# Linear attention and a two-layer product: q of the late batches transposed by DMA instead of TensorE

## The chip, the cores and the metric

The kernel runs on one core of one Trainium2 chip. The metric is the time of one execution on the device in microseconds; the kernel before takes 289.67 us (median of 3 runs, 289.25 to 289.86). The profiled execution has a span of 288.3 us, and TensorE's granted clock is 1.0 throughout.

A core has five engines that run their own instruction streams in order and meet at semaphores: TensorE (PE, matrix products into PSUM), VectorE (DVE), ScalarE (ACT), GpSimd (POOL) and SyncE (SP). Transfers between memory and the on-chip SBUF are issued from POOL, SP or ACT and carried out by 16 DMA engines that all three share. POOL's transfers can change the type on the way; here they read fp32 and write fp16.

## The reference

Eight batches of 576 tokens, 8 heads of 64. Attention without softmax, a normalisation per head, then a two-layer product with a leaky activation over all 4,608 tokens:

```python
kv = np.einsum('bhsd,bhse->bhde', k, v)
out = np.einsum('bhsd,bhde->bhse', q, kv)
rms = np.sqrt(np.mean(out * out, axis=-1, keepdims=True) + 1e-06)
attn = out / rms * g_norm                  # then (B, S, H*D) -> x: 4608 x 512
h = x @ w_in                               # 512 x 2048
g = np.maximum(h, 0.0) + alpha * np.minimum(h, 0.0)
y = g @ w_out                              # 2048 x 512
```

## The kernel before

**Windows, blocks, units.** The 4,608 tokens are cut into nine windows of 512. The loop `for w in range(1, NW)` (L731) has one block for each window from 1 to 8; window 0 is done in the start-up. A block has 16 units. In each unit TensorE computes one group of 128 hidden columns of the first layer for window w (`m1_group`, L368: four products of 512 columns), seven products of 256 columns of the second layer for window w-1 (`prod_mm`, L478; the second layer is done by a scheme with seven half-size products in place of eight), and now and then a step of the attention for window w+1 (`attention`, L713). All orders are written by hand: the schedule is manual, so each engine runs its instructions in the order in which the Python code makes them.

**Attention.** A batch has 576 tokens, a window 512, so a window touches one or two batches. Heads go in four pairs (j = 0 to 3). `step_t` (L263) transposes q of a pair: five TensorE transposes of 128x128 into a PSUM bank, then an ACT copy to SBUF (L282). `step_kv` (L284) adds up k times v over the batch's tokens into the bank "s" and DVE writes the masked result. `step_ot` (L301) multiplies k-v with the transposed q for the window's tokens; ACT squares it. `step_ssq` (L319) sums the squares and scales, giving the input `xt` of the first layer. In block w, the t step of batch w+1 stands at units 0, 3, 6 and 9, kv one unit later, ot at 3, 6, 9 and 12 and ssq two units after ot (`ATT_AT`, L701).

**Evacuation.** A first-layer group goes from PSUM through ACT (`m_sb`, L359) and DVE (`gt`, L363). From block 2 on there are two PSUM banks for the groups, so TensorE's group u+2 needs DVE to have finished group u.

**Loads.** `load_batch(w + 2)` (L731 and following) issues on POOL, for k, v and q of batch w+2: the last 64 tokens of each head (`load_rem`, L148) straight to their place in one of three sets of buffers, and the first 512 (`load_main`, L140) to a staging tile with two buffers. In the staging tile partition p holds tokens 4p to 4p+3, so each packet carries four tokens of a head: 1 KB read, 512 B written. POOL runs ahead of the loop and stops only at a load whose buffer is not free; everything behind such a load waits too.

**Regroup.** k and q are copied from the staging tile to an order in which a pair of heads is contiguous, on ACT, one pair at a time in units 8 to 15 of block w for batch w+2 (`regroup_pair`, L174; `REG_AT`, L723: q of pair j at unit 8+2j, k at 9+2j).

**Stores.** Because q holds tokens in the order 4p+t, a run of 128 result rows is spread over the output with a step of four rows, and `store_rows` (L385) cuts it where t changes or the remainder begins. Results are read from PSUM in quarters of a window (`y_read`, L509: c11 after unit 7, c22 after 11, c21 after 14, c12 in the next block's unit 0) into `y_sb`, four buffers, and stored from SP.

Of the kernel before, what the change touches and what calls it, by code (L numbers as in the profile page):

```python
# [10 lines left out]
FP16 = mybir.dt.float16  # L11
# [6 lines left out]
def kernel(  # L18
# [11 lines left out]
    nc = tc.nc  # L30

    B, H, S, D = q.shape
# [3 lines left out]
    P = 128  # L36
    NPAIR = H // 2
    W = 512
    NW = N_TOK // W
    TPW = W // P  # L40
    TPP = S // P
    MAIN = TPP * P
    REM = S - MAIN
    NT = TPP + 1
# [2 lines left out]
    NF = D_FF // P  # L47
    NC = D_MODEL // P
    assert NC == NPAIR and 0 < REM < P and P0 <= P and H % 4 == 0
    inv_d = 1.0 / D  # L50

    const_p = ctx.enter_context(tc.tile_pool(name="constp", bufs=1))
# [3 lines left out]
    stage_p = ctx.enter_context(tc.tile_pool(name="stage", bufs=2))  # L56
    attn_p = ctx.enter_context(tc.tile_pool(name="attn", bufs=2))
# [14 lines left out]
    srcs = {"q": q, "k": k, "v": v}  # L72
    st32 = {}

    def early_pair(eng, nm, tag):
# [14 lines left out]
            name=nc.get_next_instruction_name(),  # L90
# [20 lines left out]
    for r in range(P // D):  # L111
        nc.sync.dma_start(
            out=alpha_row[NF : NF + 1, r * D : (r + 1) * D], in_=g_norm[:].unsqueeze(0)
# [4 lines left out]
    NBUF = 3  # L118
    HH = H // 2
    bufs = []  # L120
    for i in range(NBUF):
        t = {}
# [6 lines left out]
    stages = {}  # L129
# [10 lines left out]
    def load_main(b, nm):  # L140
        st = stage_p.tile([P, H, TPP, D], FP16, name=f"{nm}st", tag=f"{nm}st")
        stages[b, nm] = st
        nc.gpsimd.dma_start(  # L143
            out=st[:].rearrange("p h t d -> p h (t d)"),
            in_=srcs[nm][b, :, 0:MAIN, :].rearrange("h (p t) d -> p h (t d)", t=TPP),
        )

    def load_rem(b, nm):  # L148
        nc.gpsimd.dma_start(
            out=bufs[b % NBUF][nm][0:REM, 0 if nm == "v" else TPP, :, :],  # L150
            in_=srcs[nm][b, :, MAIN:S, :].rearrange("h s d -> s h d"),
        )

    def regroup(b, nm, h0, h1, eng=None):
        dst = bufs[b % NBUF][nm][:, 0:TPP, h0:h1, :].rearrange("p t h d -> p h t d")
        src = stages[b, nm][:, h0:h1, :, :]
        if eng is nc.scalar:
            nc.scalar.copy(out=dst, in_=src)
        else:
            (eng or nc.vector).tensor_copy(out=dst, in_=src)  # L160

    def load_batch(b, names=("k", "v", "q")):
        for nm in names:
            load_rem(b, nm)
            load_main(b, nm)

    def regroup0(nm, j, n=1):
        i, h = divmod(2 * j, HH)
# [5 lines left out]
    def regroup_pair(b, nm, j):  # L174
        regroup(b, nm, 2 * j, 2 * j + 2, nc.scalar)
# [66 lines left out]
    qts, kvs, xts = {}, {}, {}  # L242

    def rows(b):
        return P0 if b == 0 else P

    def n_runs(b):
        return T0 if b == 0 else NT

    def pair_cols(b, nm, j):  # L250
        def f(t):
            n = rows(b)
            if nm == "v" and b == 0:
                h = 2 * j % HH
                return stages[b, nm, 2 * j // HH][0:n, h : h + 2, t, :]
            if nm == "v" and t < TPP:
                return stages[b, nm][:, 2 * j : 2 * j + 2, t, :]
            if nm == "v":
                return bufs[b % NBUF][nm][0:n, 0, 2 * j : 2 * j + 2, :]
            return bufs[b % NBUF][nm][0:n, t, 2 * j : 2 * j + 2, :]  # L260
        return f

    def step_t(b, j, pool=(ps_s, "s")):  # L263
        qs = pair_cols(b, "q", j)
        qt_ps = pool[0].tile([P, n_runs(b) * rows(b)], FP16, name="qt_ps", tag=pool[1])
        c = 0
        for t in range(n_runs(b)):
            n = rows(b)
            nc.tensor.matmul(  # L269
                out=qt_ps[:, c : c + n],  # L270
                lhsT=qs(t),
                rhs=ident16[0:n, 0:n],
                is_transpose=True,
                start=(t == 0),
                stop=(t == n_runs(b) - 1),
            )
            c += n
        qts[b, j] = attn_p.tile([P, S], FP16, name="qt_sb", tag=f"qt{j}")
        if b == 0 and j < 2:
            nc.vector.tensor_copy(out=qts[b, j][:], in_=qt_ps[:, 0:S])  # L280
        else:
            nc.scalar.copy(out=qts[b, j][:], in_=qt_ps[:, 0:S])  # L282

    def step_kv(b, j, pool=(ps_s, "s")):  # L284
        ks, vs = pair_cols(b, "k", j), pair_cols(b, "v", j)
# [82 lines left out]
    def m1_group(w, g, pool=None):  # L368
        h_ps = pool[0].tile([P, W], FP32, name="h_ps", tag=pool[1]) if pool else h_bank()
        m1_mm(h_ps, w, g, range(NC))  # L370
        m1_evac(h_ps, w, g)
# [4 lines left out]
    def y_mm(y, w, a, g):  # L376
        nc.tensor.matmul(  # L377
            out=y[:], lhsT=gt_cols(w, g, a * P, (a + 1) * P), rhs=w_out_blk(g),
            start=(g == 0), stop=(g == NF - 1),
        )  # L380

    store_engines = [(nc.gpsimd,)]
    store_turn = [0]

    def store_rows(n0, src, c0, c1):  # L385
        i = 0
        while i < P:
            b, r = divmod(n0 + i, S)
            np_, nt = (P0, T0) if b == 0 else (P, TPP)
            if r < np_ * nt:  # L390
                t, p = divmod(r, np_)
                cnt = min(P - i, np_ - p)
                grid = out[b * S : b * S + np_ * nt, :].rearrange("(p t) m -> t p m", t=nt)
                dst = grid[t, p : p + cnt, c0:c1]
            else:
                cnt = min(P - i, S - r)
                dst = out[b * S + r : b * S + r + cnt, c0:c1]
            engs = store_engines[0]
            store_turn[0] += 1
            engs[store_turn[0] % len(engs)].dma_start(out=dst, in_=src[i : i + cnt])  # L400
            i += cnt

    def y_out(y, w, a):
        y_sb = ysb_p.tile([P, D_MODEL], FP32, name="y_sb")
        nc.scalar.copy(out=y_sb[:], in_=y[:])
        store_rows(w * W + a * P, y_sb[:], 0, D_MODEL)


    HC = D_MODEL // 2
# [32 lines left out]
    HW = W // 2  # L442
# [60 lines left out]
        )  # L503

    def quad_out(w, r, h, src, subs=(0, 1)):
        for a in subs:
            store_rows(w * W + r * HW + a * P, src[:, a, :], h * HC, (h + 1) * HC)

    def y_read(w, what, subs=(0, 1)):  # L509
        if what == "p1":  # L510
# [47 lines left out]
    def h_at(i):  # L558
# [7 lines left out]
        out=alpha_ps[:], lhsT=alpha_row[0 : NF + 1, 0:P], rhs=ident[0 : NF + 1, 0 : NF + 1],  # L566
# [6 lines left out]
        out=beta_sb[:], in0=alpha_ps[:, 0:NF], scalar1=-1.0, scalar2=1.0, op0=ALU.mult, op1=ALU.add,  # L573
# [5 lines left out]
    regroup0("q", 1)  # L579
    keep_warm(1)  # L580
    step_t(0, 1, h_at(1))
    regroup0("k", 1)
    ssq_mm(0, 0)
# [112 lines left out]
    def unit_sums(w, u):  # L696
        for back, n, k in S_AT.get(u, ()):
            if 1 <= w + back < NW:
                s_sum(w + back, n, k)
# [13 lines left out]
    def attention(w, u):  # L713
        if w < NW:
            for what, j in (ATT_1 if w == 2 else ATT_AT).get(u, ()):
                if w < B or what in ("ot", "ssq"):
                    if w == 2 and what in ("kv", "ssq"):
                        pool = Q_POOL if j % 2 == 0 else S_POOL
                        (step_kv if what == "kv" else step_ssq)(w, j, pool)
                    else:  # L720
                        ATT[what](w, j)

    REG_AT = {8 + 2 * j + i: ((nm, j),) for j in range(NPAIR) for i, nm in ((0, "q"), (1, "k"))}  # L723

    Y3_AT = [(8, 8), (8, 8), (8, 8), (8, 9), (9, 9), (9, 10), (10, 10), (10, 10), (10, 11), (11, 11), (11, 12), (12, 12), (12, 13), (13, 14), (14, 15), (15, 16)]
    REG_2 = {
# [3 lines left out]

    for w in range(1, NW):  # L731
        if w + 2 < B:
            load_batch(w + 2)
        for u in range(NF):
            m1_group(w, G_ORDER[u])
            if w > 1:
                unit_sums(w, u)
            if w == 1 and u == 2:
                regroup(2, "k", 0, H)
            if w == 1 and u == NF - 1:  # L740
                regroup(3, "q", 0, 2)
            if w == 2 and u == 0:
                h_tags[0] = ("h1", "h2")
            if w > 2 and u == 0:
                y_read(w - 2, "c12")
            if w == 1:
                for i in range(*Y3_AT[u]):
                    y_mm(ys[3], 0, 3, i)
                    if i == NF - 1:
                        y_out(ys[3], 0, 3)  # L750
            else:
                for i in range(u * PER, (u + 1) * PER):
                    prod_mm(w - 1, *Y_LIST[i])
                for what in Y_READS.get(u, ()):
                    y_read(w - 1, what)
            attention(w + 1, u)
            if w == 1:
                for k in {5: (0,), 7: (1,)}.get(u, ()):
                    s_sum(1, 1, k)
                    s_sum(1, 2, k)  # L760
            if w + 2 < B:
                for nm, j in REG_AT.get(u, ()) if w > 1 else ():
                    regroup_pair(w + 2, nm, j)
            if w == 2:
                for nm, j in REG_2.get(u, ()):
                    regroup_pair(3, nm, j)
                if u < 2:
                    s_sum(1, u + 1, 2)
    w = NW - 1
# [47 lines left out]
```

## Time and profile before

| | share of the 288.3 us | busy us |
|---|---|---|
| PE | 97% | 280.0 |
| DVE | 77% | 220.7 |
| ACT | 61% | 176.9 |
| POOL | 17% | 50.4 |
| transposes of q on PE (L269), 164 of them | | 13.4 |
| copies of the transposed q on ACT (L282), 30 | | 18.7 |
| regroups of q on ACT (L158), 19 | | 11.7 |
| q0, POOL's DMA queue: 40,064 packets, 18.98 MB | 50.7% of 16 engines | |
| q1, SP's DMA queue: 9,396 packets, 8.24 MB | 9.7% of 16 engines | |

Busy times are sums over instructions; products are pipelined, and their ends are modelled, so a product's duration is longer than the step from its start to the next one's. What a piece of TensorE work takes is read from the starts. Idle time of an engine that isn't the bottleneck costs nothing. In such a schedule the questions are which engine has no gaps in a block, and which wait would end last if that engine had less to do.

### The profile page before, as it was taken

The numbers are of one execution on the slowest core, as the hardware profiler recorded it, in microseconds if no ns is written. First come the engines' busy times: TensorE is split into PE (matmuls) and PEld (weight loads), VectorE is DVE, ScalarE is ACT, GpSimd is POOL, SyncE is SP. The second block draws the span as 40 slices with busy tenths as digits, with TensorE's granted clock in tenths as the row PEclk, the third lists the DMA queues.
The fourth block names the chain that finished last, engine by engine and source line by source line (L and its number), as shares of the span: only waits on it lengthen the run. The fifth ranks groups of instructions, "written<-read, shape, count | busy, mean of one in ns | idle before, by whom it ended". The sixth has DMA issues, their size and how long they took to land.

```text
span 288.3 us, 5215 instructions
## 1 busy us (share of the span) xinstructions
PE 280.0 (97%) x1988; PEld 179.4 (62%) x1988; DVE 220.7 (77%) x420; ACT 176.9 (61%) x307; POOL 50.4 (17%) x72
## 2 busy tenths in 40 slices
PE   7899999999999999999999999999999999999994
PEld 2444544545666676666666766666666666666783
DVE  6569729897688877887879777877788788787862
ACT  2467448698788756886578567866754566443210
POOL 8744333751024200411020000000000000000001
PEclk9999999999999999999999999999999999999999
DMA  8999999999819990299019301120112011201223
GB/s 164 187 207 195 198 201 193 185 180 189 118 21 128 200 129 11 40 203 143 0 41 174 90 0 40 36 70 7 38 38 74 0 39 36 65 11 36 71 78 109
DMA packets 50397, 28.43 MB, mean 99 GB/s; under 512 B 13524, under 2 KB 50020, under 8 KB 50372
## 3 DMA queue, kind: packets, MB, share of 16 engines
q0 software_dynamic: 40064, 18.98, 50.7%
q1 hardware_dynamic: 9396, 8.24, 9.7%
q10 hardware_dynamic: 912, 0.89, 1.1%
q8 instruction: 15, 0.25, 0.4%
q14 instruction: 10, 0.08, 0.1%
HBM read 36.71 MB, written 9.44 MB: 160 GB/s over the span
## 4 chain that ended last, share of the span: by engine, by line
PE 87%; DMA 7%; POOL 1%; DVE 1%; issue 1%; ACT 1%; DVEq 0%; POOLq 0%
PE h_ps L352 41%; PE yY L501 15%; PE yZ L501 10%; PE yX L501 9%; DMA vst<-in_v_dram 7%; PE kv_ps L288 3%; PE ot_ps L310 3%; PE ssq_ps L326 2%; PE y L377 2%; PE qt_ps L269 2%; POOL kst L135 1%; DVE xt L336 1%; ACT rstd L328 0%; POOL vst L135 0%; POOL qst L135 0%
## 5 line engine op out<-in xcount | busy, mean ns | idle before, releaser
L352 PE MATMUL h_ps<-xt,w_in_sb 128*128 128x512 f16 x576 | 145.4, 379 | 0.4 <-DVE gt L363 0.2
L363 DVE SCALAR_TENSOR_TENSOR gt<-m_sb,beta_sb,h_ps 128x512 f16<-128x512 f32 x144 | 106.9, 746 | 45.3 <-ACT m_sb L359 43.3
L359 ACT ACTIVATE m_sb<-h_ps 128x512 f32<-128x512 f32 x144 | 86.1, 599 | 59.8 <-PE h_ps L352 47.6
L352 PEld LDWEIGHTS <-w_in_sb 128*128 128x128 f16 x576 | 54.4, 98 | 45.8 <-issue 1.3
L501 PEld LDWEIGHTS <-s 128*128 128x128 f16 x512 | 50.1, 98 | 19.3
L501 PEld LDWEIGHTS <-gt 128*128 128x128 f16 x384 | 37.6, 98 | 15.1 <-issue 0.4
L501 PE MATMUL yY<-wsum,s 128*128 128x256 f16 x256 | 36.3, 273 | 0.0
L501 PE MATMUL yX<-w_out_sb,gt 128*128 128x256 f16 x256 | 35.1, 273 | 0.1
L316 ACT ACTIVATE sq_sb<-ot_ps 128x512 f16<-128x512 f32 x36 | 21.3, 598 | 16.2 <-PE ot_ps L310 15.1
L328 ACT ACTIVATE rstd<-ssq_ps,eps_t 128x512 f32<-128x512 f32 x36 | 24.7, 690 | 9.8 <-PE ssq_ps L326 9.7
L336 DVE SCALAR_TENSOR_TENSOR xt<-ot_ps,g2col,rstd 128x512 f16<-128x512 f32 x36 | 26.5, 744 | 3.2 <-ACT rstd L328 3.2
L400 POOL DMA_DIRECT2D out_dram<-y_sb x8 | 4.4, 552 | 139.1 <-DVE y_sb L526 131.4
L282 ACT COPY qt_sb<-qt_ps 128x576 f16<-128x576 f16 x30 | 18.7, 637 | 5.8 <-PE qt_ps L269 5.8
L501 PE MATMUL yY<-wsum,gt 128*128 128x256 f16 x128 | 17.6, 273 | 0.0
L501 PE MATMUL yZ<-w_out_sb,s 128*128 128x256 f16 x128 | 17.6, 273 | 0.0
L501 PE MATMUL yZ<-wsum,s 128*128 128x256 f16 x128 | 17.6, 273 | 0.0
L377 PE MATMUL y<-w_out_sb,gt 128*128 128x512 f16 x64 | 17.1, 379 | 0.2 <-DMA w_out_sb<-in_moe_w_out_dram 0.2
L143 POOL DMA_DIRECT2D vst<-in_v_dram x7 | 6.2, 885 | 47.8 <-PE kv_ps L288 44.8
L288 PEld LDWEIGHTS <-ksb 128*128 128x128 f16 (+1 forms) x164 | 11.3, 98 | 4.9 <-DVE ksb L169 1.3
L288 PE MATMUL kv_ps<-vst,ksb 128*128 128x128 f16 (+1 forms) x136 | 12.6, 219 | 1.4 <-DMA vst<-in_v_dram 1.2
L296 DVE TENSOR_TENSOR kv_sb<-kv_ps,mask 128x128 f16<-128x128 f32 x32 | 9.1, 285 | 6.4 <-PE kv_ps L288 6.4
L310 PE MATMUL ot_ps<-qt_sb,kv_sb 128*128 128x512 f16 (+7 forms) x64 | 13.6, 286 | 0.4 <-DVE kv_sb L296 0.3
(67 smaller groups left out, 246.8 us busy)
## 6 DMA issues: line engine op xcount, KB each, us to landing
out_dram<-y_sb SPq DMA_DIRECT2D x72, 64.0 KB, 2.3
kst<-in_k_dram POOLq DMA_DIRECT2D x7, 512.0 KB, 6.9
qst<-in_q_dram POOLq DMA_DIRECT2D x7, 512.0 KB, 10.6
vst<-in_v_dram POOLq DMA_DIRECT2D x7, 512.0 KB, 9.0
out_dram<-y_sb SPq DMA_DIRECT2D x23, 128.0 KB, 2.0
w_out_sb<-in_moe_w_out_dram POOLq DMA_DIRECT2D x4, 512.0 KB, 15.8
w_in_sb<-in_moe_w_in_dram POOLq DMA_DIRECT2D x3, 512.0 KB, 12.3
w_in_sb<-in_moe_w_in_dram POOLq DMA_DIRECT2D x2, 256.0 KB, 8.5
```

The costliest lines, as they stand in the source:

```text
L282: nc.scalar.copy(out=qts[b, j][:], in_=qt_ps[:, 0:S])
L288: nc.tensor.matmul(out=kv_ps[:], lhsT=ks(t), rhs=vs(t), start=(t == 0), stop=(t == n_runs(b) - 1),)
L296: nc.vector.tensor_mul(out=kvs[b, j][:], in0=kv_ps[:], in1=mask32[:])
L310: nc.tensor.matmul(out=ot_ps[:, n0 - w * W : n1 - w * W], lhsT=kvs[b, j][:], rhs=qts[b, j][:, n0 - b * S : n1 - b * S], start=True, stop=True,
L316: nc.scalar.activation(out=sq[:], in_=ot_ps[:], func=AF.Square)
L328: nc.scalar.activation(out=rstd[:], in_=ssq_ps[:], func=AF.Abs_reciprocal_sqrt, bias=eps_t[:], scale=inv_d,)
L336: nc.vector.scalar_tensor_tensor(out=xts[w, j][:], in0=ot_ps[:], scalar=g2col[:], in1=rstd[:], op0=ALU.mult, op1=ALU.mult,)
L352: nc.tensor.matmul(out=h_ps[:], lhsT=w_in_blk(c, g), rhs=xts[w, c][:], start=(c == 0), stop=(c == NC - 1),)
L359: nc.scalar.activation(out=m_sb[:], in_=h_ps[:], func=AF.Relu, scale=-1.0)
L363: nc.vector.scalar_tensor_tensor(out=gts[w, i][:, r, :], in0=m_sb[:], scalar=beta_sb[:, g : g + 1], in1=h_ps[:], op0=ALU.mult, op1=ALU.add,)
L377: nc.tensor.matmul(out=y[:], lhsT=gt_cols(w, g, a * P, (a + 1) * P), rhs=w_out_blk(g), start=(g == 0), stop=(g == NF - 1),)
L501: nc.tensor.matmul(out=bank, lhsT=lhs, rhs=rhs, start=fresh, stop=(c == NK - 1), skip_group_check=True,)
```

## The change

For batches 4 to 7 (`B_NAT = 4`), q is not transposed by TensorE. Its main part is loaded in plain token order, one load for each run of 128 tokens (`load_q`), and after unit 11 of block w five DMA transposes issued from SP (`dma_t`) write the transposed q of batch w+2 into one tile `qt_all` for all four pairs; the attention's t step is left out for these batches, and so are q's regroups. The t step of the other batches writes a `qt_all` tile too; it has two buffers, as the tile of each pair had. The last 64 tokens of q of all late batches go to one buffer (`buf_of`: set 1) instead of one of three, so a batch's q load comes after the transposes of the batch before it; and q is loaded ahead of k and v. Since rows then stand in order, the results of these batches are stored whole: up to 256 rows in one transfer (`quad_out`, `put`). k's regroups move from units 9, 11, 13, 15 to 8, 10, 12, 14. The purpose is to take work off TensorE and ACT and to issue fewer stores.

```diff
...
     NF = D_FF // P
     NC = D_MODEL // P
     assert NC == NPAIR and 0 < REM < P and P0 <= P and H % 4 == 0
+    B_NAT = 4
     inv_d = 1.0 / D
 
     const_p = ctx.enter_context(tc.tile_pool(name="constp", bufs=1))
...
             in_=srcs[nm][b, :, 0:MAIN, :].rearrange("h (p t) d -> p h (t d)", t=TPP),
         )
 
+    def load_q(b):
+        st = stage_p.tile([P, TPP, H, D], FP16, name="qst", tag="qst")
+        stages[b, "q"] = st
+        for t in range(TPP):
+            nc.gpsimd.dma_start(
+                out=st[:, t, :, :],
+                in_=srcs["q"][b, :, t * P : (t + 1) * P, :].rearrange("h p d -> p h d"),
+            )
+
+    def buf_of(b, nm):
+        return bufs[1 if nm == "q" and b >= B_NAT else b % NBUF][nm]
+
     def load_rem(b, nm):
         nc.gpsimd.dma_start(
-            out=bufs[b % NBUF][nm][0:REM, 0 if nm == "v" else TPP, :, :],
+            out=buf_of(b, nm)[0:REM, 0 if nm == "v" else TPP, :, :],
             in_=srcs[nm][b, :, MAIN:S, :].rearrange("h s d -> s h d"),
         )
 
...
     def load_batch(b, names=("k", "v", "q")):
         for nm in names:
             load_rem(b, nm)
-            load_main(b, nm)
+            if nm == "q" and b >= B_NAT:
+                load_q(b)
+            else:
+                load_main(b, nm)
 
     def regroup0(nm, j, n=1):
         i, h = divmod(2 * j, HH)
...
                 stop=(t == n_runs(b) - 1),
             )
             c += n
-        qts[b, j] = attn_p.tile([P, S], FP16, name="qt_sb", tag=f"qt{j}")
+        if j == 0:
+            qt_all[b] = attn_p.tile([P, NPAIR, S], FP16, name="qt_all")
+        qts[b, j] = qt_all[b][:, j, :]
         if b == 0 and j < 2:
-            nc.vector.tensor_copy(out=qts[b, j][:], in_=qt_ps[:, 0:S])
+            nc.vector.tensor_copy(out=qts[b, j], in_=qt_ps[:, 0:S])
         else:
-            nc.scalar.copy(out=qts[b, j][:], in_=qt_ps[:, 0:S])
+            nc.scalar.copy(out=qts[b, j], in_=qt_ps[:, 0:S])
+
+    qt_all = {}
+
+    def dma_t(b):
+        qt = attn_p.tile([P, NPAIR, S], FP16, name="qt_all")
+        for t in range(NT):
+            c0, c1 = t * P, min((t + 1) * P, S)
+            src = stages[b, "q"][:, t] if t < TPP else buf_of(b, "q")[0:REM, TPP]
+            nc.sync.dma_start_transpose(
+                out=qt[:, :, c0:c1], in_=src.rearrange("p h d -> p (h d)"),
+            )
+        for j in range(NPAIR):
+            qts[b, j] = qt[:, j, :]
 
     def step_kv(b, j, pool=(ps_s, "s")):
         ks, vs = pair_cols(b, "k", j), pair_cols(b, "v", j)
...
     store_engines = [(nc.gpsimd,)]
     store_turn = [0]
 
+    def put(dst, src):
+        engs = store_engines[0]
+        store_turn[0] += 1
+        engs[store_turn[0] % len(engs)].dma_start(out=dst, in_=src)
+
     def store_rows(n0, src, c0, c1):
         i = 0
         while i < P:
             b, r = divmod(n0 + i, S)
+            if b >= B_NAT:
+                put(out[n0 + i : n0 + P, c0:c1], src[i:P])
+                break
             np_, nt = (P0, T0) if b == 0 else (P, TPP)
             if r < np_ * nt:
                 t, p = divmod(r, np_)
...
             else:
                 cnt = min(P - i, S - r)
                 dst = out[b * S + r : b * S + r + cnt, c0:c1]
-            engs = store_engines[0]
-            store_turn[0] += 1
-            engs[store_turn[0] % len(engs)].dma_start(out=dst, in_=src[i : i + cnt])
+            put(dst, src[i : i + cnt])
             i += cnt
 
     def y_out(y, w, a):
...
         )
 
     def quad_out(w, r, h, src, subs=(0, 1)):
+        n0 = w * W + r * HW
+        if n0 >= B_NAT * S and len(subs) == 2:
+            put(
+                out[n0 : n0 + HW, h * HC : (h + 1) * HC].rearrange("(a p) m -> p a m", p=P),
+                src[:],
+            )
+            return
         for a in subs:
-            store_rows(w * W + r * HW + a * P, src[:, a, :], h * HC, (h + 1) * HC)
+            store_rows(n0 + a * P, src[:, a, :], h * HC, (h + 1) * HC)
 
     def y_read(w, what, subs=(0, 1)):
         if what == "p1":
...
     def attention(w, u):
         if w < NW:
             for what, j in (ATT_1 if w == 2 else ATT_AT).get(u, ()):
+                if what == "t" and w >= B_NAT:
+                    continue
                 if w < B or what in ("ot", "ssq"):
                     if w == 2 and what in ("kv", "ssq"):
                         pool = Q_POOL if j % 2 == 0 else S_POOL
...
                     else:
                         ATT[what](w, j)
 
-    REG_AT = {8 + 2 * j + i: ((nm, j),) for j in range(NPAIR) for i, nm in ((0, "q"), (1, "k"))}
+    REG_AT = {8 + 2 * j: (("k", j),) for j in range(NPAIR)}
 
     Y3_AT = [(8, 8), (8, 8), (8, 8), (8, 9), (9, 9), (9, 10), (10, 10), (10, 10), (10, 11), (11, 11), (11, 12), (12, 12), (12, 13), (13, 14), (14, 15), (15, 16)]
     REG_2 = {
...
 
     for w in range(1, NW):
         if w + 2 < B:
-            load_batch(w + 2)
+            load_batch(w + 2, ("k", "v", "q") if w + 2 < B_NAT else ("q", "k", "v"))
         for u in range(NF):
             m1_group(w, G_ORDER[u])
             if w > 1:
...
             if w + 2 < B:
                 for nm, j in REG_AT.get(u, ()) if w > 1 else ():
                     regroup_pair(w + 2, nm, j)
+                if u == 11 and w + 2 >= B_NAT:
+                    dma_t(w + 2)
             if w == 2:
                 for nm, j in REG_2.get(u, ()):
                     regroup_pair(3, nm, j)
```

## The prediction

> **What bounds the kernel now.** I read the page first, then the busy time by stretch, then the timelines of single engines round the change. Columns of the table: stretch, its length, then busy time and instruction count of each engine, granted clock, DMA share, GB/s.
>
> ```profile
> PE 280.0 (97%) x1988; PEld 179.4 (62%) x1988; DVE 220.7 (77%) x420; ACT 176.9 (61%) x307; POOL 50.4 (17%) x72
> ```
> ```profile
> 99.00:129.00 30.00, 30.00 (x230) 20.62 (x229) 23.77 (x45) 21.45 (x38) 4.70 (x6) 1.00 0.69 99
> ...
> 189.00:219.00 30.00, 30.00 (x231) 20.34 (x229) 23.76 (x46) 17.88 (x30) 0.00 (x0) 1.00 0.12 33
> 219.00:246.00 27.00, 27.00 (x183) 17.61 (x181) 22.25 (x41) 15.65 (x26) 0.00 (x0) 1.00 0.13 37
> 246.00:272.00 26.00, 26.00 (x178) 17.27 (x177) 20.37 (x38) 10.51 (x18) 0.00 (x0) 1.00 0.14 42
> ```
>
> In blocks 3 to 6 (about 99 to 219 us, 30.0 us each) TensorE has no gap: 30.00 us busy of 30.00, at full clock. ACT and DVE have 8 and 6 us to spare. Blocks 7 and 8 run without transposes and k-v products and take 27 and 26 us, again with TensorE full, so the evacuation chain keeps up at that shorter unit too (26.0 / 16 = 1.63 us). The DMA engines are a third idle in blocks 3 and 4. TensorE work that leaves these blocks should therefore shorten them, unless a new wait takes its place. What one transposed pair holds is read from the starts on the PE timeline, since the busy figure 0.44 counts overlapped pipelines:
>
> ```profile
> 158.83 0.93 PE L501 MATMUL yX<-w_out_sb,gt 128*128 128x256 f16 x7
> 159.59 0.44 PE L269 MATMUL qt_ps<-ident,qsb 128*128 128x128 f16 x5
> 159.87 1.03 PE L352 MATMUL h_ps<-xt,w_in_sb 128*128 128x512 f16 x4
> ```
>
> From 159.59 to 159.87: 0.28 us for five transposes.
>
> [...] Pool's v load of the batch after next waits for its release (idle 19.0 us) and holds all loads behind it.
>
> **The change, part by part.**
>
> (1) Removed: the transposes of batches 4 to 7, 4 batches x 4 pairs x 0.28 = 4.5 us of TensorE, all in blocks 3 to 6 where it never idles. This is the gain. ACT loses 4 qt copies of 0.64 and 4 q regroups of 0.61 a batch, 5.0 us of a block's 21; it isn't the bound, so this counts as nothing by itself, but it lets ACT recover after a wait.
>
> (2) Added on SP: five transposes a batch, four of 128 KB and one of 64 KB. They are issued after unit 11's c22 store. The first waits for three things. The q load is long landed. The buffer of qt (two of them) is free once the last o product of unit 12 has read batch b-2 (92.6 us in block 2). And SP must first have issued the c22 pieces:
>
> ```profile
> 92.57 2.68 SPq L400 DMA_DIRECT2D out_dram<-y_sb  x4
> ...
> 122.58 0.87 SPq L400 DMA_DIRECT2D out_dram<-y_sb  x2
> ```
>
> So SP gets to the transposes at 95.3 in block 2 (batch 4), 1.8 us earlier relative to the block in block 3 (two pieces), and late again in block 4 (four pieces). In block 5 c22 is one whole store. The c21 store behind them slips by some 5 us, with four y_sb buffers and over 10 us before its buffer is wanted: nothing.
>
> Time from there to the last landing, T: at the least five plain issues (0.58 us, median of SP's 96 stores, four whole steps) and a store's landing 2.3 us after the fifth starts: 4.6 us. [...] I take 1.2 each, and 2.5 us from the fifth's start to its landing: T = 7.3 us. [...]
>
> (3) Who waits for T? First, the o product of the next block's unit 3 (at 105.0 in block 3, 104.8 without the first transposes): 95.3 + 7.3 = 102.6, so 2.2 us to spare. Second, and tighter, the loads. The remainder rows of q of all late batches now use one buffer, so q(b+1) may be loaded only when the transposes of b have read it; q goes first, and k and v stand behind it on Pool. K of batch 5 is wanted by ACT in unit 8 of block 3, where the q regroup stands now:
>
> ```profile
> 115.34 0.69 ACT L328 ACTIVATE rstd<-ssq_ps,eps_t 128x512 f32<-128x512 f32 x1 [0.38 <-PE ssq_ps L326]
> 115.92 0.61 ACT L158 COPY qsb<-qst 128x512 f16<-128x512 f16 x1
> 116.43 0.60 ACT L359 ACTIVATE m_sb<-h_ps 128x512 f32<-128x512 f32 x1
> ```
>
> Three removed pairs earlier, it is wanted at 115.1. ACT waits there in order, with m_sb of unit 9 behind it. TensorE has two h banks and stops first at unit 11, now 119.2 - 1.1 = 118.1: k copy 0.5, m_sb 0.6 and gt 0.75 must precede, so a landing up to 116.3 costs nothing; each later us costs one.
>
> (4) The load time. Q in token order comes in pieces of 64 elements: 4 x 1,024 packets of 128 B instead of 1,024 of 512 B, plus 512 of the remainder as before.
>
> ```profile
> kst<-in_k_dram POOLq DMA_DIRECT2D x7, 512.0 KB, 6.9
> ...
> ksb<-in_k_dram POOLq DMA_DIRECT2D x7, 64.0 KB, 10.2
> ```
>
> The 128 B remainder packets last 32 ns each in the packet records and the 512 B ones 60, but they overlap: at full flow 192 of the large go in 0.5 us (2.6 ns each over all engines), of the small about one per 1.1 ns; one after the other on sixteen engines they would take 32 / 16 = 2.0. From the issue of a first load to full flow the records show 3.2 us, with 0.6 us of work done by then. Q: 4,608 x 1.3 ns (between) = 6.0. K: 1,024 x 2.6 + 512 x 1.3 ns = 3.3. Two 256 KB stores among them 1.5, receipt 0.7. Sum 3.2 - 0.6 + 6.0 + 3.3 + 1.5 + 0.7 = 14.1 us; 12.5 at the fast end, 17.5 at 2.0 ns. K lands at 95.3 + 7.3 + 14.1 = 116.7: 0.4 us late in batch 5, in time in batch 6 (1.8 us earlier), 0.4 late in batch 7. Batch 4's loads stand behind no transpose. Pool issues five loads of 0.7 to 0.9 us in place of two, below the transfer: hidden.
>
> (5) Whole stores: fewer issues on SP. The last store of the kernel becomes one of 128 KB on SP for two of 64 on SP and ACT; same bytes, and two Pool stores leave the tail. I give it 0 to 0.3 us, and count 0.1.
>
> Sum: 289.67 - 4.5 - 0.1 + 0.8 = 285.9 us; 285.1 if k is in time; I say **285.7**.
>
> **Rivals.**
> A (chance 0.60): the forecast, stalls of 0 to 2 us in all, 285.0 to 287. For it: every block is full of TensorE work, and the rest fits.
> B (0.15): T is about 9.5 us or the small packets run at 1.7 ns, k is late by some 2 in batches 5 and 7 and 0.3 in 6: +4.3, which eats the gain: 287 to 290. For it: the margin in (3) is nil.
> C (0.25), slower: T 11 us or more. K late by 11 - 7.3 + 0.4 = 4.1, 2.3 and 4.1: +10.5 - 4.6 = 295.6; with both costs at their ends over 300. [...] For it: SP's transposes are the one price the trace doesn't have, and loads of 20 us are put behind them. [...]
>
> **Numbers.** Within 0.2% is 289.1 to 290.2, a fifth of B: faster 0.60 + 0.12 = 0.72, same 0.03, slower 0.25. The range leaves C's far half out above: 284.8 to 292.5.
>
> **What would show it.** Blocks 3 to 6 at 28.9 us with TensorE full and no qt_ps after 93 us: (1) right. Transposes on SP starting at 95.3, last landing near 102.6: T. An ACT wait on a k load at unit 8, and a gap of TensorE three units later: the stall, its size the difference of the two. Wrong above all if one transpose holds SP for 2 us or more, or small packets flow at 2 ns.

## The result, and the profile after

The changed kernel takes 285.67 us (median of 4 runs, 283.91 to 286.47) against 289.76 before (289.25 to 289.87), a ratio of 0.985 with a 95% interval of 0.981 to 0.990. Its profiled execution, with 286.47 us the slowest of the four, has a span of 284.6 us. The single times lie 2.6 us apart, those of before 0.6.

The page after, and its busy time by stretch (the late blocks are now 28.9 us long, so the stretches are cut anew):

```profile
PE 275.9 (97%) x1908; PEld 174.9 (61%) x1908; DVE 220.3 (77%) x420; ACT 160.7 (56%) x275; POOL 59.4 (21%) x82
```
```profile
99.00:128.00 29.00, 27.55 (x199) 18.33 (x197) 22.10 (x44) 16.39 (x29) 7.32 (x9) 1.00 0.90 122
128.00:157.00 29.00, 29.00 (x211) 19.54 (x210) 23.75 (x47) 17.49 (x31) 7.31 (x9) 1.00 0.85 111
157.00:186.00 29.00, 29.00 (x211) 19.45 (x210) 23.73 (x46) 17.60 (x32) 7.32 (x9) 1.00 0.92 127
186.00:215.00 29.00, 29.00 (x211) 19.31 (x210) 23.89 (x46) 15.99 (x28) 0.00 (x0) 1.00 0.18 45
```

TensorE has 80 products fewer and fills blocks 4, 5 and 6 as it did before. Block 3 is not full: 27.55 of 29.00. Where the 1.45 us went is read in three timelines of the same stretch. First SP's and Pool's:

```profile
94.89 5.89 SPq L309 DMA_TRANSPOSE qt_all<-qst  x4
100.87 1.20 SPq L309 DMA_TRANSPOSE qt_all<-qsb  x1
```
```profile
103.78 0.69 POOL L162 DMA_DIRECT2D qsb<-in_q_dram  x1 [34.56 <-DVE gt L394]
104.46 3.52 POOL L153 DMA_DIRECT2D qst<-in_q_dram  x4
107.93 0.73 POOL L162 DMA_DIRECT2D ksb<-in_k_dram  x1
108.61 0.94 POOL L144 DMA_DIRECT2D kst<-in_k_dram  x1
```

The five transposes of batch 4 occupy SP from 94.89 to 102.07; Pool, idle since its last load, goes on at 103.78. The profile puts this 34.56 us wait down to a DVE instruction that had long been done: the q load waits for two semaphores, and the release that fits in time is the last transpose landing. (In the two later blocks the table of waits does name it: `qsb` from the transpose of `qsb`, 44.5 us in two waits, and Pool's issue follows the landing by some 0.5 us.) K's main load is issued at 108.61 and lands 8.6 us later. Then ACT and TensorE:

```profile
114.33 0.69 ACT L359 ACTIVATE rstd<-ssq_ps,eps_t 128x512 f32<-128x512 f32 x1 [0.38 <-PE ssq_ps L357]
117.20 0.62 ACT L171 COPY ksb<-kst 128x512 f16<-128x512 f16 x1 [2.18 <-DMA kst<-in_k_dram]
117.73 0.59 ACT L390 ACTIVATE m_sb<-h_ps 128x512 f32<-128x512 f32 x1
```
```profile
117.60 0.39 PE L319 MATMUL kv_ps<-vst,ksb 128*128 128x128 f16 x4
117.83 0.22 PE L319 MATMUL kv_ps<-vsb,ksb 128*128 128x128 f16 x1
119.15 1.02 PE L383 MATMUL h_ps<-xt,w_in_sb 128*128 128x512 f16 x4 [1.10 <-DVE gt L394]
...
121.28 0.39 PE L357 MATMUL ssq_ps<-sq_sb,mask 128*128 128x512 f16 x1 [0.35 <-DVE kv_sb L327]
```

ACT wants k at 115.0, gets it at 117.20; TensorE stops at unit 11 for 1.10 us and at its end for another 0.35. Of the 2.18 us that ACT waited, 0.73 did not reach TensorE as idle time.

The account of the span, from the starts on TensorE: from the beginning of block 2 to the last product before takes 214.33 us, after 211.65, of which 1.45 are gaps. (The beginning is here the start of the block's second product group; a wait of at least 0.18 us just before it stands in every profile.) Without the gaps it is 2.68 + 1.45 = 4.1 us shorter; a version without gaps, below, gives 4.46. The missing 0.33 belongs to the stall too: idle time is counted from a product's modelled end, and each of the two interruptions also loses about 0.16 us of the overlap between products. From its first product to that of the next block, block 3 takes 30.68 us and blocks 4 to 6 take 28.89, so the stall cost 1.8 us in all. From the last product to the end takes 4.13 us before and 3.28 after. The rest is the start, where block 2 begins at 69.85 before and at 69.68 after.

### The profile page after: what moved, and what is told of

It reads as the page before. It is cut to its first block, busy times and chain, and to the rows that moved or that the text cites. A ratio compares the mean times of both kernels' runs of the same rounds, so it can differ in the third digit from the quotient of the medians.

```text
span 284.6 us, 5030 instructions
## 1 busy us (share of the span) xinstructions
PE 275.9 (97%) x1908; PEld 174.9 (61%) x1908; DVE 220.3 (77%) x420; ACT 160.7 (56%) x275; POOL 59.4 (21%) x82
## 3 DMA queue, kind: packets, MB, share of 16 engines
q1 hardware_dynamic: 18836, 10.67, 13.4%
## 4 chain that ended last, share of the span: by engine, by line
PE 76%; DMA 15%; DVE 3%; POOL 2%; issue 1%; ACT 1%; POOLq 0%; DVEq 0%; ACTq 0%
PE h_ps L383 36%; PE yY L538 13%; PE yZ L538 9%; PE yX L538 8%; DMA vst<-in_v_dram 5%; DMA w_in_sb<-in_moe_w_in_dram 5%; DMA kst<-in_k_dram 3%; PE kv_ps L319 2%; PE y L408 2%; PE ot_ps L341 2%; PE ssq_ps L357 2%; DMA qst<-in_q_dram 2%; DVE gt L394 1%; POOL qst L153 1%; ACT m_sb L390 1%
## 5 line engine op out<-in xcount | busy, mean ns | idle before, releaser
L162 POOL DMA_DIRECT2D qsb<-in_q_dram x7 | 4.9, 702 | 81.1 <-DMA qt_all<-qsb 44.5
L153 POOL DMA_DIRECT2D qst<-in_q_dram x16 | 14.1, 901 | 0.3 <-DMA out_dram<-y_sb 0.3
L357 PE MATMUL ssq_ps<-sq_sb,mask 128*128 128x512 f16 x36 | 13.6, 379 | 0.6 <-DVE kv_sb L327 0.3
L341 PE MATMUL ot_ps<-qt_all,kv_sb 128*128 128x512 f16 (+7 forms) x64 | 13.6, 286 | 0.4 <-DVE kv_sb L327 0.3
L490 DVE TENSOR_TENSOR s<-s,gt 128x512 f16<-128x512 f16 x32 | 13.5, 421 | 0.5
L171 ACT COPY ksb<-kst 128x512 f16<-128x512 f16 x20 | 12.3, 615 | 2.2 <-DMA kst<-in_k_dram 2.2
```

The lines of the kernel that those rows point to most:

```text
L153: nc.gpsimd.dma_start(out=st[:, t, :, :], in_=srcs["q"][b, :, t * P : (t + 1) * P, :].rearrange("h p d -> p h d"),)
L341: nc.tensor.matmul(out=ot_ps[:, n0 - w * W : n1 - w * W], lhsT=kvs[b, j][:], rhs=qts[b, j][:, n0 - b * S : n1 - b * S], start=True, stop=True,
L357: nc.tensor.matmul(out=ssq_ps[:], lhsT=mask16[:], rhs=sq[:], start=True, stop=True)
```

## The experiments

All ran beside the kernel before on the same chip (289.5 to 289.7 us). "Middle" is the time from the beginning of block 2 to the last product in the profiled execution, "gaps" the idle time of TensorE in it, "tail" the time from there to the end; the start isn't in either, and varies: in the profiles of this study with batch 3 as before, block 2 begins between 69.3 and 70.3 us.

| kernel | us, median (lowest to highest) | ratio to before, 95% | middle | gaps in it | tail |
|---|---|---|---|---|---|
| before | 289.76 | | 214.33 | 0 | 4.13 |
| changed | 285.67 (283.91 to 286.47) | 0.981 to 0.990 | 211.65 | 1.45 | 3.28 |
| changed, again | 286.44 (286.13 to 287.34) | 0.987 to 0.991 | 211.08 | 0.70 | 3.27 |
| k regrouped a unit later | 284.83 (284.05 to 285.34) | 0.981 to 0.985 | 210.36 | 0.32 | 3.27 |
| k and v loaded first | 284.59 (284.18 to 285.15) | 0.981 to 0.984 | 209.87 | 0 | 3.28 |
| own remainder buffers | 284.43 (284.22 to 284.75) | 0.980 to 0.984 | 209.87 | 0 | 3.27 |
| transposes ahead of c22 | 284.28 (284.15 to 284.78) | 0.980 to 0.983 | 209.87 | 0 | 3.27 |
| the last two together | 284.81 (284.09 to 285.53) | 0.981 to 0.986 | 209.87 | 0 | 3.27 |
| TensorE transposes | 289.00 (288.41 to 289.89) | 0.997 to 0.999 | 214.33 | 0 | 3.55 |
| three transposes more | 301.86 (298.84 to 302.89) | 1.035 to 1.046 | 226.71 | 11.97 | 3.55 |
| last stores cut | 286.32 (285.77 to 286.62) | 0.986 to 0.990 | 211.06 | 0.86 | 3.87 |
| batch 3 as well | 284.22 (283.11 to 284.80) | 0.978 to 0.982 | | 0.89 in block 2 | 3.22 |

**The changed kernel again.** Expected: 

> The changed kernel once more, on the chip of the three beside it. 285.7 us, with single times spread over 2 us (283.9 to 286.5). If the k load's lateness in block 3 is what spreads them, its profile shows an ACT wait on kst between 0 and 3 us and a TensorE gap of about 1.1 us less than that wait; if something else does, gaps stand elsewhere.

It came out at 286.44. ACT waits twice on k, 2.0 us in all with 1.2 the longer; TensorE's gaps are 0.16 and 0.34 us in block 3 and 0.20 in block 5. So the gap comes and goes with the moment at which k lands. It isn't the whole spread: this profile has 0.75 us less of gaps than the first, and the same span, because its block 2 began 0.6 us later. What moves the start isn't shown.

**Where the gain comes from: TensorE transposes.** The late batches are transposed by TensorE again, from the staging tile in token order, and their remainder rows get the buffers of before.

```diff
-        return bufs[1 if nm == "q" and b >= B_NAT else b % NBUF][nm]
+        return bufs[b % NBUF][nm]
...
+            if nm == "q" and b >= B_NAT:
+                if t < TPP:
+                    return stages[b, nm][:, t, 2 * j : 2 * j + 2, :]
+                return buf_of(b, nm)[0:n, t, 2 * j : 2 * j + 2, :]
...
-                if what == "t" and w >= B_NAT:
-                    continue
...
-                if u == 11 and w + 2 >= B_NAT:
-                    dma_t(w + 2)
```

> No DMA transposes: TensorE transposes q of batches 4 to 7 straight from the staging tile in token order, each batch with its own remainder buffer. Loads in small packets, whole stores and the missing q regroups stay. Theory (the gain is 16 x 0.28 us of TensorE): blocks 3 to 6 back at 30.0 us, only the shorter tail of the stores (0.85 us) is kept, 288.8 us. Rival (the gain comes from a lighter ACT or from whole stores): 286 or less.

289.00: nothing is left of the gain but the tail. ACT is relieved of the q regroups, the stores are whole and there is no gap, yet the middle is 214.33 us as before, to the hundredth. The first product groups of blocks 4 and 5 show it, here and (second pair) in the version below that loads k and v first:

```profile
127.46 1.03 PE L387 MATMUL h_ps<-xt,w_in_sb 128*128 128x512 f16 x4
157.47 1.03 PE L387 MATMUL h_ps<-xt,w_in_sb 128*128 128x512 f16 x4
```
```profile
126.29 1.03 PE L383 MATMUL h_ps<-xt,w_in_sb 128*128 128x512 f16 x4
155.18 1.03 PE L383 MATMUL h_ps<-xt,w_in_sb 128*128 128x512 f16 x4
```

A block takes 30.01 us with TensorE's transposes and 28.89 without. The gain is TensorE's time; a lighter ACT and fewer stores brought nothing in the blocks.

**Where the gap comes from: four ways to take it away.** Each touches one link of the chain from c22's stores over the transposes, q and k to ACT.

K later wanted:

```diff
-    REG_AT = {8 + 2 * j: (("k", j),) for j in range(NPAIR)}
+    REG_AT = {9 + 2 * j: (("k", j),) for j in range(NPAIR)}
```

> k's regroups back at units 9, 11, 13, 15: k is wanted about 1.9 us later, nothing else changes. Theory (what is left of a stall is ACT waiting for the k load behind the transposes): the TensorE gap in block 3 (1.45 us in the first profile) goes, 284.3 us, and the times lie closer together. Rival (the gap comes from the transposes' own traffic or from DVE): still 285.7.

284.83. ACT still waits 0.7 us once; 0.32 us of gap is left, at unit 11 in the sum of squares. Counted from unit 8, k came 2.5 us late in this run (114.80 to 117.27), and the edit gives it 1.75.

K no longer behind q:

```diff
-            load_batch(w + 2, ("k", "v", "q") if w + 2 < B_NAT else ("q", "k", "v"))
+            load_batch(w + 2, ("k", "v", "q"))
```

> Late batches load k, v, q in that order, so k no longer stands behind the transposes; q still does. Theory: no wait of ACT on kst, no gap of TensorE in blocks 3 to 6, 284.3 us as with the later regroup. Rival (the lateness is of the DMA engines as a whole, not of the order): 285.7 or worse, since q now comes last.

284.59, no gap, no wait on k. The stretch that had lost 1.45 us:

```profile
99.00:128.00 29.00, 29.00 (x211) 19.61 (x210) 23.68 (x46) 17.44 (x31) 7.33 (x9) 1.00 0.95 128
```

The DMA share is even higher there (0.95 for 0.90), and TensorE is full: the load on the DMA engines isn't what it waited for.

Q no longer behind the transposes:

```diff
-        return bufs[1 if nm == "q" and b >= B_NAT else b % NBUF][nm]
+        return bufs[b % NBUF][nm]
```

> The last 64 tokens of q of late batches go to the set of their batch (one of three) again, so no load waits for the transposes of the batch just before. Order q, k, v as in the changed kernel. Theory: Pool loads batch 5 during block 2, k is there long before unit 8 of block 3, no TensorE gap, 284.4 us as with k and v first. Rival (the loads collide with the transposes and the stores when the gate is gone): transposes of well over 1.3 us each, and 286 or more.

284.43, no gap. Pool now waits for transposes only at the staging tile, for the batch two before (21.7 us in two waits). Beside the loads a transpose held SP for 1.22 us in the median and 2.30 at worst.

The transposes earlier, ahead of unit 11's `y_read` and so of c22's stores:

```diff
+                if u == 11 and w + 2 < B and w + 2 >= B_NAT:
+                    dma_t(w + 2)
                 for what in Y_READS.get(u, ()):
                     y_read(w - 1, what)
...
-                if u == 11 and w + 2 >= B_NAT:
-                    dma_t(w + 2)
```

> The five transposes are issued ahead of the c22 store of unit 11; gate and order stay. Theory: in block 2 they start at 93.1 us, when the last o product is done, in place of 94.9, so k comes 1.8 us earlier and the gap of block 3 (0.5 to 1.5 us in two profiles) goes: 284.6 us. c22's pieces wait some 7 us on SP and cost nothing. Rival (stores held up by the transposes come back as a wait for y_sb buffers): 287 or more, with waits on y_sb.

284.28, no gap, though ACT still waits 0.3 us once for k. The first transpose starts at 92.84 us, and no wait on `y_sb` appears beyond those that the changed kernel has.

Two of these together:

> Own remainder buffers and the transposes ahead of c22's store together. Theory (each of the two alone has already taken away all of the gap of block 3, and nothing else of TensorE is left over): no better than either alone, 284.3 us. Rival (each removes a part of a larger cost): 283.5 or less.

284.81, with the same middle, 209.87, as each alone. What they remove is one and the same gap; in the profiles the four gapless kernels have the same middle and tail and differ by the start alone.

**What a later end of the transposes costs.**

```diff
+        for t in range(3):
+            nc.sync.dma_start_transpose(
+                out=bufs[2]["q"][:, t].rearrange("p h d -> p (h d)").rearrange("p (a c) -> p a c", c=P),
+                in_=stages[b, "q"][:, t].rearrange("p h d -> p (h d)"),
+            )
         qt = attn_p.tile([P, NPAIR, S], FP16, name="qt_all")
```

> Three more transposes of 128x512, from the same staging tile into a dead buffer, ahead of the five of each late batch: 3.9 us more on SP. Theory (each us by which the transposes end later costs a us of TensorE once the slack is gone): gaps of about 4.6 to 5.4 us in block 3, 2.3 in block 4 and 2.7 in block 5, 295 us. Rival (the load gate is not what ties the transposes to TensorE): 286 us.

301.86, and so 16 us more than the changed kernel, where the way from the first transpose to Pool's next load grew by 4.1 us in block 2. ACT and TensorE in block 3:

```profile
120.84 0.62 ACT L171 COPY ksb<-kst 128x512 f16<-128x512 f16 x1 [6.18 <-DMA kst<-in_k_dram]
```
```profile
117.47 0.22 PE L324 MATMUL kv_ps<-vsb,ksb 128*128 128x128 f16 x1
122.79 1.86 PE L388 MATMUL h_ps<-xt,w_in_sb 128*128 128x512 f16 x4 [5.11 <-DVE gt L399]
124.45 0.84 PE L543 MATMUL yZ<-wsum,s 128*128 128x256 f16 x3
```

The idle times are 5.11 us in block 3, 4.31 in block 4, and 2.20 with another 0.35 behind it in block 5, 11.97 in all; expected were 4.6 to 5.4, 2.3 and 2.7. Blocks 3 and 5 came out as said; block 4's is nearly double. Before it Pool issued its next load 4.2 us after the start of the last transpose (137.12 to 141.28), before the other two 2.8. That is 1.3 us of the difference; its cause stays open.

The forecast of 295 missed what follows the gaps: four products that take 0.87 us elsewhere take 1.66 (122.79 to 124.45). The clock fell.

```profile
122.40:125.70 3.30, 2.91 (x10) 1.43 (x10) 2.84 (x7) 1.64 (x4) 0.00 (x0) 0.50 0.08 11
156.50:163.20 6.70, 5.61 (x18) 2.57 (x18) 5.31 (x10) 3.10 (x7) 0.00 (x0) 0.50 0.14 22
191.70:200.00 8.30, 7.95 (x52) 4.84 (x52) 7.54 (x16) 5.16 (x10) 0.00 (x0) 1.00 0.28 73
```

The column before the DMA share is the granted clock. It was 0.50 from 122.33 us for 3.4 us after the gap of 5.11, 0.50 from 156.46 for 6.8 us after the gap of 4.31, and 1.00 after the gap of 2.20. TensorE worked again from 122.79 and 157.59, so it had 2.95 and 5.70 us at half clock and lost half of that, 4.3 us. The middle has 226.71 - 209.87 - 11.97 = 4.9 beyond the gaps; the rest is about what four interruptions lose of the overlap, 0.16 us each. The shorter of the two gaps cost more clock, so its length alone doesn't set the loss.

**The tail.** The last window's stores in pieces of 64 rows, on the queues of before.

```diff
+        if w == NW - 1:
+            for a in subs:
+                for i in (0, 64):
+                    put(out[n0 + a * P + i : n0 + a * P + i + 64, h * HC : (h + 1) * HC], src[i : i + 64, a, :])
+            return
```

> The changed kernel with the last window's results stored in pieces of 64 rows as before, on the same queues as before, Pool among them. Theory (the 0.85 us by which the end came closer to the last product is from the whole stores): from the last product to the end 4.1 us again in place of 3.3, so 0.85 us longer, 286.9. Rival (the shorter end has another source, as fewer semaphores to wait for): no change.

The tail is 3.87 us, 0.6 longer than with whole stores; the median, 286.32, can't be told from the 286.44 of the changed kernel on another chip, since the gap in block 3 (0.86 here) and the start move it by as much. The traces show where it goes. The last store lands 2.24 us after the last product in the changed kernel, 2.83 in this one: whole stores with Pool left out shortened the end by some 0.6 us. The kernel with TensorE's transposes, whole stores too, has a tail of 3.55 although its last store lands at 2.27. The other 0.3 lies behind the landing. SP closes the program by waiting for its semaphores of transfers one after the other, some 0.06 us each, and there the last store's stands third of nine, with six waits behind it; in the changed kernel it stands seventh. With three transposes more it is third again and the tail 3.55; with one batch more, below, it is eighth and the tail 3.22. In the kernel before, the wait for the last landing ended at 3.0 us and was the fifth, so the 0.26 us from 3.87 to 4.13 are a later landing and two more waits. The rival of fewer waits at the end thus holds for a small part.

**One batch more.** `B_NAT = 3`, with own remainder buffers, and batch 3's q regroups left out.

> Batch 3 too has its q transposed by DMA (in block 1), with own remainder buffers; q of batch 3 is loaded in token order ahead of k and v. Theory: block 2 loses 4 x 0.28 = 1.12 us of TensorE and nothing waits, if the transposes, which start near 64 us while the weights' and batches' loads still fill the DMA engines, land before the o product of unit 3 of block 2 near 75 us: 283.3 us. Rival (in full DMA traffic the transposes or k of batch 3 come late): a gap of TensorE in block 2, 285 or more.

284.22 (283.11 to 284.80), between the two. SP issues batch 3's transposes from 63.85 to 71.5 us, in the fullest DMA traffic (174 GB/s between 39 and 69 us, 170 between 69 and 98), with 2.0 us for the slowest; they land only 8.0 to 9.0 us after their issue, the last at 78.3. The o product of unit 3, which needs three of the five, is held by about 0.2 us at 75.7. V of batch 3 comes 0.43 us late, and a wait for DVE is 0.46 us instead of the usual 0.18. From its first product to that of block 3, block 2 takes 30.53 us against 30.59 in the kernel before, so nearly all of the 1.12 us goes again.

On the chip on which the changed kernel ran again, two versions, the one with k regrouped later and the one with k and v first, beat it clearly (284.83 and 284.59 against 286.44). The other gapless ones and this one ran on other chips; their ratios to before lie below that of this second run, and overlap with the first run's and with one another's.

## Why the prediction was right

**The bound and step (1), right.** "TensorE work that leaves these blocks should therefore shorten them": predicted 16 x 0.28 = 4.5 us, measured 214.33 - 209.87 = 4.46 wherever no gap is left in blocks 3 to 6 and block 2 is as before, and nothing at all where TensorE keeps the transposes. Reading 0.28 us from the starts was what made it right; the busy figure of 0.44 us would have promised 7.

**Step (2), nearly right.** SP got to the transposes at 94.9 us (95.3 said). Four of the five held SP for 1.2 to 1.3 us, the second of batch 4 for 1.87; from start to start it was 1.31 as a rule. T was to end with the last landing: from the first transpose that was 7.6 us for batch 5 and 8.3 for batch 6, for 7.3 said (batch 4's last landing isn't recorded). Between the landing and Pool's next issue another 0.5 us passes, which the prediction had at nothing, so to that issue it was 8.9, 8.1 and 8.8 us. The prediction's 1.2 us for one transpose, and with it T and the 11 us of rival C, were its author's estimates: before's trace has no DMA transpose to read them from. The trace after has 1.22 in the median of the sixteen of 128x512. The bytes were not the limit: the packets of five transposes, 2,304 of 256 B, last 18 ns each, 2.6 us over 16 engines in all, estimated from these figures, where SP was occupied for 7.2 (94.89 to 102.07). The 19.0 us wait that the prediction names was Pool waiting for a k-v product to free a buffer; Pool waiting for another DMA is what the changed kernel shows, 23.75 us for the transposes before its load in block 5.

**Step (3), right in the link, wrong in one waiter.** K behind q behind the transposes is the tighter wait, ACT stands at unit 8, and TensorE stops at unit 11. Predicted landing 116.7, 0.4 us over the slack; found 117.2, with 1.10 us of gap, and 0.35 behind it, 1.8 in all from start to start where 0.4 was said. In block 4 there was none, as said; in block 5 none and 0.20 in two profiles where 0.4 was said. The o product of unit 3, named as the first waiter, does not wait for T. In the kernel with three transposes more it ran at 104.21 us in block 3, before the fifth transpose was issued (104.65): for window 4 it reads 256 tokens of batch 4, so the first two transposes and not all five.

**Step (4), right in sum.** From Pool's issue to k it was 13.4 us in block 3, 13.3 in block 4 and 11.3 in block 5, for 14.1 (12.5 to 17.5) said. (With its own 1.1 and 2.0 ns the sum gives 13.1 and 17.7.) Small packets flowed faster than taken: up to 596 in half a microsecond, 0.84 ns each for 1.3, in packets that last 32 ns; so at that pace, an estimate, more than two are under way at once on each of 16 engines.

**Step (5), too small.** 0.1 us counted, 0.85 measured in the tail, of which some 0.6 is the earlier landing of the last store.

So the way to Pool's next issue was taken too short by 0.8 to 1.6 us and the load too long by 0.7 to 3, which nearly cancel, and the tail makes up for the larger stall: 289.67 - 4.46 + 1.78 - 0.85 = 286.1 with the stall of the first profile (211.65 - 209.87), 285.6 with the 1.21 of the second (211.08 - 209.87), where 0.8 and 0.1 had been counted for stall and tail. The mechanism was right in each link but the unit-3 waiter; that the sum hits so well is in part luck, as the run-to-run spread of 2.6 us shows.

Rival C was no phantom: with the way to Pool's next issue at 13.0 us (94.53 to 107.48, in the kernel with three more) it came to pass, and with a loss of clock on top, of which before's trace, at 1.00 throughout, shows nothing. In the kernel with three more, the gaps of 4.31 and 5.11 us were followed by a granted clock of 0.50, that of 2.20 by 1.00. The clock fell 3.2 and 4.6 us after the modelled end of the last product before the two.

## What to carry to other kernels

Work taken off the full TensorE was worth its step from start to start here (16 x 0.28 us = 4.5, measured 4.46), and all of it was kept only where the transfer that replaces it had slack at its next waiter (a middle of 209.87 us, against 211.65 with the stall). Follow the buffer that such a transfer frees, since in this kernel that sets when the next load may begin and who stands behind it: Pool went on at 103.78 us, after transposes that held SP until 102.07. A load that nobody needs early should not stand ahead of one with a date: another order of the loads, a buffer of its own or an earlier start of the transposes each gave back the whole gap here (1.45 us in the first profile, 0.70 in the second), a unit's delay all but 0.32. In these runs a gap of up to 2.2 us cost its length and some 0.16 us; the two of 4.3 and 5.1 us, after which the clock fell to 0.50, cost nearly half as much again (14.0 us for 9.4 of idle time).

## What the runs showed of the hardware that was not expected

A transposing DMA held SP for about 1.2 us per 128x512 block of fp16 (1.22 in the median, 1.19 to 1.87 in the changed kernel) and as long for one of 64x512 (1.20), at 2.3 us in the median from issue to landing; in the fullest traffic, with batch 3 as well, it was 8 to 9 us. Loads in packets of 128 B moved up to one per 0.84 ns, those of 512 B up to one per 2.6. At these paces, an estimate, the same 512 KB in quarter packets are 4,096 x 0.84 = 3.4 us of flow in place of 1,024 x 2.6 = 2.7, a third more and not four times. The end of the program moved with the place of the last store's semaphore in SP's row of waits: 3.55, 3.27 and 3.22 us of tail with it third, seventh and eighth, for landings within 0.04 us of each other.
